# Sliding-window attention beside an MLP: row maxima by 64 queries of two heads and 320 keys, with the zeros in q's stacks

## The chip, the cores and the metric

One core of a Trainium2 chip runs the whole program. Its engines are TensorE (PE: matmuls; PEld: the loads of its weights), VectorE (DVE), ScalarE (ACT), GpSimd (POOL) and SyncE (SP), whose queue issues every DMA here. The metric is the device time of one execution in microseconds (us); several executions are timed and their median is given.

## The reference

Two branches read the same x (2048 tokens, 512 features) and are mixed by a gate per token.

```python
def _A_ref(x, wqkv, wo):
    B, S, D = x.shape
    H = 32; Dh = D // H; W = 256
    qkv = (lambda x, *d: x.transpose(*d))((x @ wqkv).reshape(B, S, 3, H, Dh), 2, 0, 3, 1, 4)
    q, k, v = qkv[0], qkv[1], qkv[2]
    scores = jnp.einsum("bhqd,bhkd->bhqk", q, k) * (Dh ** -0.5)
    idx = jnp.arange(S)
    mask = (idx[:, None] - idx[None, :] >= 0) & (idx[:, None] - idx[None, :] < W)
    scores = jnp.where(mask[None, None], scores, -1e9)
    p = _softmax(scores, axis=-1)
    o = jnp.einsum("bhqk,bhkd->bhqd", p, v)
    return (lambda x, *d: x.transpose(*d))(o, 0, 2, 1, 3).reshape(B, S, D) @ wo

def _B_ref(x, w1, b1, w2, b2):
    h = _gelu(jnp.einsum("bsd,df->bsf", x, w1) + b1)
    return jnp.einsum("bsf,fd->bsd", h, w2) + b2

g = _sigmoid((x * gate_w).sum(-1, keepdims=True))
return g * _A_ref(A_x, A_wqkv, A_wo) + (1 - g) * _B_ref(A_x, B_w1, B_b1, B_w2, B_b2)
```

A query sees its own key and the 255 before it. There are 32 heads of 16 features; the MLP has 1792 hidden units.

## The kernel before, in words

*Precision.* Matmul operands are float32r, each value as a high and a low part. `mm3` (lines 89 to 92) multiplies high by high, high by low and low by high. Attention does the same with one matmul by stacking: q and k of a head are 48 rows, 16 features each of (high, low, high) in one and of (high, high, low) in the other, in the order that `load_stack` brings them from scratch tensors SQ and SK in DRAM, one of each for every 512 tokens ("chunk").

*Heads.* A group is four heads, handled as two pairs (`pr`) of two (`s`). Rows 0 to 47 of the stacks belong to the pair's first head, rows 48 to 95 to its second. In the kernel before, `qs` holds both heads' q on top of one another, and `ks` holds each head's k apart, with zeros in the other head's 48 rows (`ks[:, pr, s]`). A matmul of the 96 rows so gives the scores of the one head whose k it takes.

*Maxima.* `att_max(g_, b, i)` (L377) computes, for 128 queries of one head, the scores against up to 384 keys (tile `sm`, three PSUM buffers), and `red` (L382) has DVE add a mask and take the maximum of each row into `M`, in one instruction whose elementwise output `jm` is thrown away. A second small instruction reads the maximum out. For every four blocks of 128 queries (`RB`), `att_rows` negates the maxima on DVE, as a high and a low part, transposes them (L393 to L397), and POOL copies them by `put` (L402) into rows 96 to 103 of `qs`. Ones in rows 96 to 103 of `ks`, written by `clear_k` from `own`, pick the two rows of the own head, so that the next matmul of the scores has the maximum already subtracted.

*Weights of attention.* `att_exp` (L417) takes 128 keys as the stationary operand and up to 384 queries as the moving one (tile `st`), ACT takes the exponential (L429), and POOL zeroes what lies outside the window (L421, L424). `att_pv` (L449) multiplies by v. Its result goes to DRAM (ND, L461), the normaliser is loaded, inverted and applied for each pair of groups (`att_norm`: den, num, RD, rb, OT), and the output projection follows at the end.

*Order.* PE, ACT, DVE and POOL run in the order in which the program is written; each engine takes its instructions in turn. A clock kept while the program is written (`now`, `tick`, `after`) decides that order: `after(ns, f)` puts `f` so many model nanoseconds later. The main loop (from line 700) goes over blocks u of 128 keys in all 8 groups, 16 to a group. The maxima run `LEAD` = 8 blocks ahead of the exponentials. In each of four turns of a block it writes one maximum, one matmul of weights and about 574 ns of dense work (QKV projections at first, then the MLP), by `fill`. DMAs stand on SP's queue in an order that the tile framework's scheduler makes; each uses one of eight semaphores in turn. Every fourth block, `att_load` brings the next chunk of q and k, over the place whose last reader is the matmul of weights eight blocks behind. The MLP's input is brought back by `load_x` (tile `mx`, L501), the weights as `raw`.

*Start.* While the QKV projections of the first three chunks run, `ks` and `qs` serve as buffers of the transposed x; `clear_k` and `load_k` then prepare `ks` piece by piece, and q follows at line 698.

Of the kernel before, what the change touches and what calls it, by code (L numbers as in the profile page):

```python
# [9 lines left out]
F32 = mybir.dt.float32  # L10
F32R = mybir.dt.float32r
BF16 = mybir.dt.bfloat16
AF = mybir.ActivationFunctionType
# [19 lines left out]
def gated_mix(ctx: ExitStack, tc: tile.TileContext, x, wqkv, wo, w1, b1, w2, b2, gate_w, out):  # L33
# [11 lines left out]
    def f32(ap):  # L45
        return ap.bitcast(F32)

    idle = sb.tile([128, 384], BF16, tag="jm", bufs=1, name="idle")
# [18 lines left out]
    mask = cp.tile([128, 384], BF16, name="mask")  # L67
    nc.gpsimd.memset(mask, 0.0)
    nc.gpsimd.affine_select(out=mask[:, 0:128], in_=mask[:, 0:128], pattern=[[1, 128]],
                            compare_op=ALU.is_ge, fill=NEG, base=-1, channel_multiplier=-1)  # L70
    nc.gpsimd.affine_select(out=mask[:, 256:384], in_=mask[:, 256:384], pattern=[[-1, 128]],
                            compare_op=ALU.is_ge, fill=NEG, base=0, channel_multiplier=1)

    own = cp.tile([128, 4], F32, name="own")
    nil = cp.tile([128, 1], F32, name="nil")
    nc.gpsimd.memset(nil, 0.0)
    nc.gpsimd.memset(own, 0.0)
    for k in (0, 1):
        nc.gpsimd.affine_select(out=own[96:104], in_=own[96:104], pattern=[[-2, 4]], compare_op=ALU.not_equal,
                                fill=1.0, base=-k, channel_multiplier=1)  # L80
    nms = cp.tile([128, RB, 32], F32R, name="nm")
# [3 lines left out]
    z = cp.tile([128, S // 128], F32, name="z")  # L85
# [99 lines left out]
    def qkv_x(t, b):  # L185

        if b == 0:
            if t < NT - 1:
                v = (ks[:, 0], ks[:, 1], qs)[t].rearrange("p a c -> p (a c)")
# [25 lines left out]
    def gate_end(t):  # L215
        sl = slice(t * NB, (t + 1) * NB)
        nc.scalar.activation(g1[:, sl], z[:, sl], AF.Exp, scale=-1.0)
# [4 lines left out]
    def gate_z(t, b):  # L222
# [3 lines left out]
        nc.vector.tensor_tensor_reduce(junk, xr, gwb, 1.0, 0.0, ALU.mult, ALU.add, z[:, nb:nb + 1])  # L226
# [48 lines left out]
    def qkv(t):  # L275
# [17 lines left out]
        for n, (kind, j) in enumerate(pieces):  # L293
# [15 lines left out]
            if t == 1 and n % 3 == 2:  # L309
                clear_k(n // 3)  # L310
            if t == 2 and n in (1, 3, 5, 7):
                clear_k(4 + n // 2)
# [456 lines left out]
```

## Time and profile before

| what | value |
|---|---|
| median of 3 timed runs | 789.53 us (787.77 to 789.83) |
| the profiled execution | 789.78 us |
| its span | 788.1 us |
| granted TensorE clock, mean | 0.995 |
| share of the span: PE, PEld, DVE, ACT, POOL | 97, 78, 66, 54, 46% |
| DMA packets | 97085, 139.66 MB |

A matmul's record goes from its start to the end of its last result, and the next one starts before that end; busy PE time is thus an upper bound on work, and distances between starts are the price. "jm", "sm", "st", "nm", "tt" are the program's tile names; L and a number is a line of the kernel. A row of a group gives the line, the engine, the operation, output<-input, partitions x elements, the count, then busy us, mean ns of one, and the idle time before it with what ended it.

### The profile page before, as it was taken

What the parts mean: (1) busy time and instruction counts of PE and PEld (TensorE: products, weight loads), DVE (VectorE), ACT (ScalarE), POOL (GpSimd) and SP (SyncE); (2) the same over time, 40 slices, a digit from 0 to 9 for tenths busy, and PEclk for the clock granted to TensorE, in tenths of its full rate; (3) what the DMA queues carried; (4) which work ended last, traced back from release to release, by engine and by line L of the source; (5) the groups of instructions that cost most, each with busy time, mean ns of one, the idle gap of its engine ahead of it and who ended that gap; (6) DMA issues with size and microseconds to landing.
All of it is one profiled execution on the core that took longest, in us unless ns stands there. A gap on an engine that the chain in (4) does not pass through costs nothing.

```text
span 788.1 us, 14535 instructions
## 1 busy us (share of the span) xinstructions
PE 768.1 (97%) x4630; PEld 618.5 (78%) x4630; DVE 521.6 (66%) x1516; ACT 429.0 (54%) x865; POOL 363.6 (46%) x701
## 2 busy tenths in 40 slices
PE   8999999989999999999999999999999999999997
PEld 5888888867888878788868867878888888777776
DVE  4533333888568857966996799668867966791353
ACT  4424433356467546755774577457646754775640
POOL 2200000047457745754765467447744863685100
PEclk9999999999999999999999999999999999999999
DMA  9985856637552653573335556533664364345882
GB/s 292 362 299 189 302 189 202 229 108 256 153 134 69 213 176 113 183 205 115 106 109 161 168 148 191 156 91 109 199 202 137 94 228 129 116 135 177 257 294 94
DMA packets 97085, 139.66 MB, mean 177 GB/s; under 512 B 32496, under 2 KB 44016, under 8 KB 97008
## 3 DMA queue, kind: packets, MB, share of 16 engines
q1 hardware_dynamic: 97008, 138.72, 55.8%
q8 instruction: 37, 0.61, 0.3%
q14 instruction: 40, 0.33, 0.1%
HBM read 83.63 MB, written 55.05 MB: 176 GB/s over the span
## 4 chain that ended last, share of the span: by engine, by line
PE 66%; DVE 5%; issue 4%; DMA 2%; ACT 2%; POOL 1%; DVEq 0%; POOLq 0%; SPq 0%
PE pv L449 10%; PE st L417 9%; PE sm L377 9%; PE y L90 7%; PE y L91 6%; PE y L92 6%; PE u L90 5%; PE u L91 4%; PE u L92 4%; DVE jm L382 2%; PE a L92 1%; DVE sqh L541 1%; PE a L90 1%; PE a L91 1%; DMA ND<-nd 1%
## 5 line engine op out<-in xcount | busy, mean ns | idle before, releaser
L382 DVE CUSTOM_DVE_ANT_0 jm<-sm,mask 128x384 bf16<-128x384 f32 (+2 forms) x512 | 269.5, 526 | 121.0 <-PE sm L377 94.2
L429 ACT ACTIVATE pt<-st 128x384 f32<-128x384 f32 (+2 forms) x512 | 232.5, 473 | 148.3 <-PE st L417 142.1
L421 POOL TENSOR_SCALAR_AFFINE_SELECT pt<-pt 128x256 f32<-128x256 f32 x256 | 117.4, 459 | 184.0 <-ACT pt L429 177.9
L377 PE MATMUL sm<-ks,qs 96*128 96x384 f32 (+2 forms) x512 | 171.2, 336 | 8.7 <-DVE M L382 7.7
L417 PE MATMUL st<-qs,ks 128*128 128x384 f32 (+2 forms) x512 | 169.2, 332 | 0.9 <-ACT pt L429 0.9
L377 PEld LDWEIGHTS sm<-ks,qs 96*128 96x128 f32 x512 | 96.8, 189 | 37.5 <-DVE M L382 19.5
L417 PEld LDWEIGHTS st<-qs,ks 128*128 128x128 f32 x512 | 97.6, 191 | 18.7 <-ACT pt L429 1.5
L424 POOL TENSOR_SCALAR_AFFINE_SELECT pt<-pt 128x256 f32<-128x256 f32 x224 | 102.5, 457 | 0.0
L553 POOL TENSOR_TENSOR h<-x1h,h 128x512 fp32r<-128x512 f32 x56 | 81.8, 1460 | 37.2 <-DVE h L550 29.4
L90 PE MATMUL y<-w,h 128*128 128x512 f32 x224 | 89.8, 401 | 0.0
L402 POOL CAST qs<-tt 8x256 fp32r<-8x256 f32 x128 | 64.7, 505 | 50.7 <-PE u L92 38.8
L91 PE MATMUL y<-w,h 128*128 128x512 f32 x224 | 88.0, 393 | 0.0
L92 PE MATMUL y<-w,h 128*128 128x512 f32 x224 | 88.0, 393 | 0.0
L449 PE MATMUL pv<-pt,vbuf 128*32 128x384 f32 (+2 forms) x1408 | 84.3, 386 | 0.0
L90 PE MATMUL u<-mx,w 128*128 128x512 f32 x196 | 79.1, 404 | 0.0
L91 PE MATMUL u<-mx,w 128*128 128x512 f32 x196 | 76.6, 391 | 0.0
L92 PE MATMUL u<-mx,w 128*128 128x512 f32 x196 | 76.5, 390 | 0.0
L449 PEld LDWEIGHTS pv<-pt,vbuf 128*32 128x32 f32 x1408 | 41.5, 110 | 41.8 <-issue 29.1
L245 DVE TENSOR_TENSOR qke<-qk,qke 128x512 fp32r<-128x512 f32 x32 | 22.1, 690 | 49.7 <-ACT qke L242 48.1
L460 ACT ACTIVATE nd<-pv 128x512 f32<-128x512 f32 x32 | 19.2, 598 | 60.1 <-PE pv L449 57.9
L242 ACT ACTIVATE qke<-qk 128x512 fp32r<-128x512 f32 x32 | 19.2, 599 | 57.7 <-PE qk L92 43.1
L92 PEld LDWEIGHTS y<-w,h 128*128 128x128 f32 x224 | 42.3, 189 | 9.4
(116 smaller groups left out, 1231.5 us busy)
## 6 DMA issues: line engine op xcount, KB each, us to landing
mx<-XT SPq DMA_DIRECT2D x24, 512.0 KB
SQ<-qke SPq DMA_DIRECT2D x16, 512.0 KB
SK<-qke SPq DMA_DIRECT2D x16, 512.0 KB
qs<-SQ SPq DMA_DIRECT2D x64, 128.0 KB
ND<-nd SPq DMA_DIRECT2D x32, 256.0 KB
ks<-SK SPq DMA_DIRECT2D x60, 128.0 KB
raw_w<-in_B_w_dram SPq DMA_DIRECT2D x28, 256.0 KB
SV<-vx SPq DMA_DIRECT2D x16, 272.0 KB
```

The lines of the kernel that those rows point to most:

```text
L90: nc.tensor.matmul(p, lh, rh, start=first, stop=False)
L91: nc.tensor.matmul(p, lh, rl, start=False, stop=False)
L92: nc.tensor.matmul(p, ll, rh, start=False, stop=last)
L377: nc.tensor.matmul(p[:, :w], qs[0:96, pr, b * 128:(b + 1) * 128], ks[0:96, pr, s, k0:k0 + w], start=True, stop=True)
L382: nc.vector.tensor_tensor_reduce(junk[:, :w], p[:, :w], mask[:, 384 - w:384], 1.0, -3e38, ALU.add, ALU.max, M[:, b % RB, i:i + 1])
L402: nc.gpsimd.tensor_copy(dst, tt[32 * i:32 * i + 8].unsqueeze(1).broadcast_to([8, 2, RB, 32]))
L417: nc.tensor.matmul(p[:, :w], ks[:, pr, s, kb * 128:(kb + 1) * 128], qs[:, pr, kb * 128:kb * 128 + w], start=True, stop=True)
L421: nc.gpsimd.affine_select(out=pt[:, :, 0:128], in_=pt[:, :, 0:128], pattern=[[0, 2], [1, 128]], compare_op=ALU.is_ge, fill=0.0, base=0, ch ...
L424: nc.gpsimd.affine_select(out=pt[:, :, 256:384], in_=pt[:, :, 256:384], pattern=[[0, 2], [-1, 128]], compare_op=ALU.is_ge, fill=0.0, base= ...
L429: nc.scalar.activation(pt[:, s, :w], p[:, :w], AF.Exp, scale=SCALE)
L449: nc.tensor.matmul(pv[32 * i:32 * i + 32, q - c * T:e - c * T], vt[:, 68 * (kb % NB) + 17 * i:68 * (kb % NB) + 17 * i + 32], pts[g_, kb, i ...
L553: nc.gpsimd.tensor_sub(h[:, 1], x1, f32(h[:, 0]))
```

## The change

The zeros move from k's stacks to q's. `ks` now holds both heads' k on top of one another, `[128, 2, S]`, and `qs` is `[128, 2, 2 * S]`: for every 64 queries it has 64 columns of the one head and 64 of the other, with zeros in the other head's rows. In a block of 128 queries the four runs of 64 columns are second head, first head, first head, second head, so that the first head's 128 columns lie together and the second head's in two runs.

`att_max` takes 128 such columns, that is 64 queries of both heads, as the stationary operand, and up to 320 keys as the moving one. There are as many of these matmuls as before. The mask is 320 wide, in two halves of partitions. `M`, `nm` and `tt` are by 64 queries and two pairs, and `put` copies 4 partitions of 512 elements where it copied 8 of 256. `att_exp` takes k of both heads in 100 rows, and picks the head by the columns of q: two runs of 64 columns out of every 256 for the second head. The ones in rows 96 to 99 of `ks` are written once, by two copies on POOL.

q is brought by `load_q`, for one pair and one head at a time: two DMAs with runs of 128 columns for the first head, four for the second (runs of 128, and of 64 at both ends). A chunk so has 12 DMAs of q where it had 4; k keeps 4 and now follows q. At the start q is loaded early and k at the end, the other way round from before.

Besides, the thrown-away output is a fixed tile of bytes, `M` and `den` have one buffer in place of two, the gate's sums lie in `g1`, and `att_rows` is due 50 model ns after its last maximum, not 900.

```diff
...
-    mask = cp.tile([128, 384], BF16, name="mask")
+    mask = cp.tile([128, 320], BF16, name="mask")
...
+    junk = cp.tile([128, 320], U8, name="junk")
...
+    nil = own[:, 2:3]
...
-    nms = cp.tile([128, RB, 32], F32R, name="nm")
+    nms = cp.tile([128, RB * 2, 32], F32R, name="nm")
...
-    qs = cp.tile([128, 2, S], F32R, name="qs")
-    ks = cp.tile([128, 2, 2, S], F32R, name="ks")
-
-    def clear_k(i):
+
+    qs = cp.tile([128, 2, 2 * S], F32R, name="qs")
+    ks = cp.tile([128, 2, S], F32R, name="ks")
+
+    def clear_q(i):
 
         pr, n = divmod(i, 4)
-        v = ks[:, pr].rearrange("p s c -> p (s c)")
-        c = 2 * pr + n // 2
-        nc.scalar.activation(v[:, n * 1024:(n + 1) * 1024], nil.broadcast_to([128, 1024]), AF.Identity,
-                             bias=own[:, c:c + 1])
+        nc.scalar.activation(qs[:, pr, n * 1024:(n + 1) * 1024], nil.broadcast_to([128, 1024]), AF.Identity, bias=nil)
...
-    def load_k(g_, c, prs):
+    def load_stack(src, high, put):
+
+        put(0, src.rearrange("d s c -> (d s) c"))
+        put(32, src[:, high])
+
+    def load_q(g_, c, prs):
+
+        need(("qk", c, g_ // 2))
+        for pr in range(prs.start, prs.stop):
+            v = f32(qs[:, pr, 2 * c * T:2 * (c + 1) * T])
+
+            def put_a(r, src):
+                dst = v[r:r + src.shape[0]].rearrange("r (n x) -> r n x", x=256)[:, :, 64:192]
+                nc.sync.dma_start(dst, src.rearrange("r (n x) -> r n x", x=128))
+
+            def put_b(r, src):
+                w = v[48 + r:48 + r + src.shape[0]]
+                nc.sync.dma_start(w[:, 192:960].rearrange("r (n x) -> r n x", x=256)[:, :, 0:128],
+                                  src[:, 64:448].rearrange("r (n x) -> r n x", x=128))
+                nc.sync.dma_start(w.rearrange("r (n x) -> r n x", x=64)[:, 0:16:15],
+                                  src.rearrange("r (n x) -> r n x", x=64)[:, 0:8:7])
+            load_stack(SQ[c][4 * g_ + 2 * pr], 1, put_a)
+            load_stack(SQ[c][4 * g_ + 2 * pr + 1], 1, put_b)
+
+    def att_load(g_, c, k_only=False):
         need(("qk", c, NC + g_ // 2))
         cs = slice(c * T, (c + 1) * T)
+        if not k_only:
+            load_q(g_, c, slice(0, 2))
         for s in range(2):
-            heads = slice(4 * g_ + 2 * prs.start + s, 4 * g_ + 2 * prs.stop - 1 + s, 2)
-            load_stack(SK[c], 0, heads, lambda r, n: ks[48 * s + r:48 * s + r + n, prs, s, cs])
...
+            src = SK[c][4 * g_ + s:4 * g_ + 3 + s:2]
+            nc.sync.dma_start(f32(ks[48 * s:48 * s + 32, :, cs]), src.rearrange("h d s c -> (d s) h c"))
+            nc.sync.dma_start(f32(ks[48 * s + 32:48 * s + 48, :, cs]), src[:, :, 0].rearrange("h d c -> d h c"))
...
     def att_max(g_, b, i):
...
-        k0 = max(b - 2, 0) * 128
-        w = (b + 1) * 128 - k0
-        pr, s = divmod(i, 2)
+        pr, half = i % 2, i // 2
+        k = 2 * b + half
+        w = min(W + 64, 64 * k + 64)
+        k0 = 64 * k + 64 - w
         p = ps.tile([128, 384], F32, tag="sm", bufs=3, name=f"sm{g_}_{b}_{i}")
-        nc.tensor.matmul(p[:, :w], qs[0:96, pr, b * 128:(b + 1) * 128], ks[0:96, pr, s, k0:k0 + w],
-                         start=True, stop=True)
...
+        nc.tensor.matmul(p[:, :w], qs[0:96, pr, k * 128:(k + 1) * 128], ks[0:96, pr, k0:k0 + w], start=True, stop=True)
         def red():
...
-            nc.vector.tensor_tensor_reduce(junk[:, :w], p[:, :w], mask[:, 384 - w:384], 1.0, -3e38,
-                                           ALU.add, ALU.max, M[:, b % RB, i:i + 1])
+            if b % RB == 0 and i == XOR:
+                Ms[g_, b // RB] = sb.tile([128, RB * 2, 2], F32, tag="M", bufs=1, name=f"M{g_}_{b}")
+            M = Ms[g_, b // RB]
+            nc.vector.tensor_tensor_reduce(junk[:, :w], p[:, :w], mask[:, 320 - w:320], 1.0, -3e38,
+                                           ALU.add, ALU.max, M[:, b % RB * 2 + half, pr:pr + 1])
...
         def put(i):
-            dst = qs[96:104, :, rb * RB * 128:(rb + 1) * RB * 128]
-            dst = dst.rearrange("r s (b i j) -> r s b i j", b=RB, i=4)[:, :, :, i]
-            nc.gpsimd.tensor_copy(dst, tt[32 * i:32 * i + 8].unsqueeze(1).broadcast_to([8, 2, RB, 32]))
+            dst = qs[96:100, :, rb * RB * 256:(rb + 1) * RB * 256]
+            dst = dst.rearrange("r s (b i j) -> r s b i j", i=4, j=32)[:, :, :, i]
+            nc.gpsimd.tensor_copy(dst, tt[32 * i:32 * i + 4].unsqueeze(1).broadcast_to([4, 2, RB * 2, 32]))
...
-        nc.tensor.matmul(p[:, :w], ks[:, pr, s, kb * 128:(kb + 1) * 128],
-                         qs[:, pr, kb * 128:kb * 128 + w], start=True, stop=True)
+        q = qs[0:100, pr, kb * 256:kb * 256 + 2 * w].rearrange("r (b u j) -> r b u j", u=4, j=64)
+        q = q[:, :, 0:4:3] if s else q[:, :, 1:3]
+        nc.tensor.matmul(p[:, :w], ks[0:100, pr, kb * 128:(kb + 1) * 128], q, start=True, stop=True)
...
-        den = sb.tile([128, 32], F32, tag="den", bufs=2, name=f"den{t}_{c}")
+        den = sb.tile([128, 32], F32, tag="den", bufs=1, name=f"den{t}_{c}")
...
     need(("v", NT - 2, NB - 1))
+    for pr in range(2):
+        nc.gpsimd.tensor_copy(ks[96:100, pr], own[96:100, pr:pr + 1].broadcast_to([4, S]))
     att_load(*chunks.pop(0), True), att_load(*chunks.pop(0), True)
...
-            after(900, att_rows, gm, bm // RB)
+            after(50, att_rows, gm, bm // RB)
```

More of the change, by code (lines that the diff above doesn't have):

```diff
@@ L12 @@
 BF16 = mybir.dt.bfloat16
+U8 = mybir.dt.uint8
 AF = mybir.ActivationFunctionType
@@ L46, in f32 @@
         return ap.bitcast(F32)
-    idle = sb.tile([128, 384], BF16, tag="jm", bufs=1, name="idle")
+    idle = sb.tile([128, 384], BF16, tag="ya", bufs=2, name="idle")
     nc.gpsimd.memset(idle, 0.0)
@@ L225, in gate_z @@
         nb = t * NB + b
-        nc.vector.tensor_tensor_reduce(junk, xr, gwb, 1.0, 0.0, ALU.mult, ALU.add, z[:, nb:nb + 1])
+        nc.vector.tensor_tensor_reduce(junk, xr, gwb, 1.0, 0.0, ALU.mult, ALU.add, g1[:, nb:nb + 1])
     def qkv_qk(t, j):
@@ L337, in gated_mix @@
     vts, Ms, pts, pvs = {}, {}, {}, {}
-    def load_stack(src, high, heads, rows):
-        nc.sync.dma_start(f32(rows(0, 32)), src[heads].rearrange("h d s c -> (d s) h c"))
-        nc.sync.dma_start(f32(rows(32, 16)), src[:, :, high][heads].rearrange("h d c -> d h c"))
-    def load_k(g_, c, prs):
+    def load_stack(src, high, put):
[16 more added lines that the diff above has]
+            load_stack(SQ[c][4 * g_ + 2 * pr + 1], 1, put_b)
```

43 lines of the change are left out of this document (14 added, 29 removed).

## The prediction

> **What bounds the kernel now.** I began with the page's busy shares, then cut the span into windows, then read the tensor engine's start times one by one.
>
> ```profile
> span 788.1 us, 14535 instructions
> PE 768.1 (97%) x4630; PEld 618.5 (78%) x4630; DVE 521.6 (66%) x1516; ACT 429.0 (54%) x865; POOL 363.6 (46%) x701
> ```
>
> The profiled execution took 789.78 us, 1.7 more than its span; the three timed runs have a median of 789.53. The sum below is made against 789.8.
>
> ```profile
> 130.00:735.00 605.00, 594.54 (x3822) 478.44 (x3824) 453.01 (x1389) 361.62 (x753) 351.46 (x664) 0.99 0.51 155
> 175.00:180.00 5.00, 3.93 (x16) 2.95 (x17) 4.57 (x12) 3.79 (x9) 4.82 (x9) 1.00 0.50 157
> 405.00:410.00 5.00, 3.65 (x17) 2.62 (x15) 5.00 (x11) 3.24 (x8) 4.81 (x7) 1.00 0.54 150
> 410.00:415.00 5.00, 4.55 (x15) 3.85 (x16) 4.20 (x14) 2.58 (x5) 2.28 (x6) 0.70 0.16 54
> 455.00:485.00 30.00, 27.97 (x183) 20.01 (x181) 28.75 (x74) 21.76 (x44) 21.20 (x33) 1.00 0.46 133
> ```
>
> These are windows; the columns are busy PE, PEld, DVE, ACT, POOL, then granted clock, DMA share, GB/s. From 130 to 735 us, the whole attention stage, PE is busy 594.5 of 605 us: whatever shortens a matmul there shortens the kernel. The exceptions are short. At 405 to 410 DVE is busy all 5.00 us and PE 3.65; then the clock is granted at 0.70. Between 455 and 485 DVE is busy 28.75 of 30. At 175 to 180 POOL is at 4.82 of 5.
>
> A busy matmul overlaps its neighbours, so its price is the distance from its start to the next start:
>
> ```profile
> 219.82 0.34 PE L377 MATMUL sm<-ks,qs 96*128 96x384 f32 x1
> 222.92 0.34 PE L377 MATMUL sm<-ks,qs 96*128 96x384 f32 x1
> 779.85 0.39 PE L90 MATMUL a<-wo,ot 128*128 128x512 f32 x1
> 781.89 0.28 PE L90 MATMUL a<-wo,ot 128*128 128x256 f32 x1
> 783.93 0.28 PE L92 MATMUL a<-wo,ot 128*128 128x256 f32 x1
> 204.17 0.22 PE L377 MATMUL sm<-ks,qs 96*128 96x128 f32 x1
> 204.23 0.40 PE L417 MATMUL st<-qs,ks 128*128 128x384 f32 x1
> ```
>
> Nine 512-column matmuls go from 779.85 to 781.89: 0.2267 us each. Seventeen of 256 columns go from there to 783.93: 0.120. Three rounds of one sm, one st and three 512s go from 219.82 to 222.92, 1.033 each; less 3 x 0.2267 that leaves 0.353, or 0.1766 for each 384-column matmul. A 128-column sm takes 0.06. So cost grows by 0.06 per 128 columns with no floor at these sizes, although each has a 128-column weight load.
>
> **The change, part by part.** The order of PE's instructions is unchanged, the new kernel issues as many matmuls, and each sm or st streams fewer columns or as many. The rows are groups by line, shapes apart: count | busy us, mean ns | idle before, and what ended it.
>
> ```profile
> L377 PE MATMUL sm<-ks,qs 96*128 96x384 f32 x448 | 154.9, 347 | 8.7 <-DVE M L382 7.7
> L377 PE MATMUL sm<-ks,qs 96*128 96x256 f32 x32 | 9.1, 283 | 0.0
> L377 PE MATMUL sm<-ks,qs 96*128 96x128 f32 x32 | 7.3, 227 | 0.0
> L382 DVE CUSTOM_DVE_ANT_0 jm<-sm,mask 128x384 bf16<-128x384 f32 x448 | 247.0, 551 | 88.3 <-PE sm L377 63.7 <-PE st L417 0.5
> L382 DVE CUSTOM_DVE_ANT_0 jm<-sm,mask 128x256 bf16<-128x256 f32 x32 | 13.5, 423 | 10.2 <-PE sm L377 9.2
> L402 POOL CAST qs<-tt 8x256 fp32r<-8x256 f32 x128 | 64.7, 505 | 50.7 <-PE u L92 38.8
> L82 POOL MEMSET nm<- 128x128 f32 x1 | 0.2, 205 | 0.1
> L84 POOL MEMSET vbuf<- 128x32 f32 x1 | 0.1, 125 | 0.0
> ```
>
> 1. *sm shrinks.* Now: 448 x 0.1766 + 32 x 0.120 + 32 x 0.06 = 84.9 us. After: 448 of 320 columns at 0.148, half way between 0.120 and 0.1766, plus 16 each of 64, 128, 192 and 256 columns, 0.30 us for such a set: 66.3 + 4.8 = 71.1. **Gain 13.8 us, on the path.** The points lie within 2 ns of a line, so 13 to 15; zero if 320 were charged like 384.
>
> 2. *st reads q in runs.* Its 384 columns are now three runs of 128 for even heads, six of 64 for odd ones, and 100 rows in place of 128. No row shows a moving operand in runs. Lower end: 0, only the count matters (128-row st and 96-row sm cost the same now); no gain below that, since the columns are the same. Next, three runs at 0.06 are 0.18: 3.4 ns more, 1.7 us over 512. Upper end: a run of 64 costs as the shortest stream seen, 0.06: six are 0.36, 0.183 more for each of 256 odd-head matmuls, 47 us. I take 1, the 384-column row being nearest, and the far end as a rival.
>
> 3. *The reductions shrink.* 320 elements interpolate to 487 ns, 64 below 551: 448 x 0.064 = 28.7 us of DVE. PE covers nearly all of it; it pays only where DVE sets the pace. There 64 ns are saved where PE saves 29, so 35 ns more per reduction: about 100 reductions in the windows around 175, 400, 470 and 700 give 3.5 us, against PE's whole wait on reductions of 7.7 us above. **I take 3;** bounds 0 and 9 (7.7 plus half of a clock window such as that after 410). The bytes in place of bf16 for the thrown-away result, and one M buffer, which DVE alone writes and reads in order, I cost at nothing; DVE's own order covers them.
>
> 4. *POOL's casts double per partition,* from 8x256 to 4x512. Bounds 505 ns (partitions counted not at all, fixed cost all) and 1010 (all by element); the two memsets give 80 ns for 96 elements, so a fixed part of some 100, and doubling the other 405 gives 910; I take 900. That is 128 x 0.4 = 51 us, to about 403 of 605 us in the stage: covered, except where POOL's queue stands on the chain of waits:
>
> ```profile
> 174.01 0.75 POOL qs L402
> 178.22 1.26 POOL h L553
> 179.51 0.69 ACT x1h L535
> ```
>
> The casts of rows sit ahead of the subtraction at 178.22, for which ACT's gelu waits, and behind it PE's next u. Four casts there, 0.4 each: **1.6 us lost**, between 0 and 2.
>
> DVE and POOL also hold each other up:
>
> ```profile
> 394.81 0.68 DVE L149 TENSOR_TENSOR w<-raw_w,w 128x512 fp32r<-128x512 f32 x1
> 407.28 1.28 POOL L553 TENSOR_TENSOR h<-x1h,h 128x512 fp32r<-128x512 f32 x1
> 407.33 1.78 DVE L149 TENSOR_TENSOR w<-raw_w,w 128x512 fp32r<-128x512 f32 x1
> ```
>
> The same DVE subtraction takes 0.68 alone and 1.78 when it starts beside POOL's at 407.28. So longer casts can hand part of the 28.7 us back; if all 51 us of them fell on DVE, point 3 would be zero or a loss. [...]
>
> 5. *Loads.* Per group and 512-token chunk, k keeps its 4 DMAs; q goes from 4 to 12, all on SP's queue, q now first. The two chunks loaded early go the same way. With 8 more issues, everything behind them on SP (k, V, normaliser and MLP loads) comes later. A window, SP's and PE's timelines, and a step of the chain of waits (the time from issue to landing):
>
> ```profile
> 180.00:185.00 5.00, 4.77 (x23) 3.66 (x22) 4.57 (x15) 4.52 (x11) 3.90 (x7) 1.00 0.78 294
> 185.13 2.28 SPq L501 DMA_DIRECT2D mx<-XT  x4
> 192.05 0.32 SPq L461 DMA_DIRECT2D ND<-nd  x1
> 192.41 0.43 SPq L342 DMA_DIRECT2D ks<-SK  x1
> 193.84 0.98 SPq L341 DMA_DIRECT2D qs<-SQ  x1
> 194.87 0.43 SPq L342 DMA_DIRECT2D qs<-SQ  x1
> 195.34 0.42 SPq L341 DMA_DIRECT2D qs<-SQ  x1
> 196.34 0.30 SPq L342 DMA_DIRECT2D qs<-SQ  x1
> 332.12 0.32 SPq L461 DMA_DIRECT2D ND<-nd  x1
> 336.74 0.30 SPq L342 DMA_DIRECT2D qs<-SQ  x1
> 344.24 0.22 PE L377 MATMUL sm<-ks,qs 96*128 96x128 f32 x1
> 459.59 2.85 DMA raw_w<-in_B_w_dram
> ```
>
> An issue takes 0.47 (194.87 to 195.34); a load of short runs lands in 2.85. Chunk 4's last load starts at 196.34, lands by about 199.2, and is first used at 204.17: margin 5.0 us. Chunk 12: 336.74, 339.6, 344.24: 4.6. Eight more issues are 3.8, so most chunks keep about a microsecond. At chunk 4 more moves: the four mx loads, now ahead of ND, stand behind it. They start near 192.5, and 2.1 MB at the 294 GB/s of the window is 7 us, to about 200; a load waits until the one eight before it has landed (eight DMA semaphores go round), so six issues and a landing follow, 205.7, where PE wants them near 202.7 (204.17 less what sm has saved). **3 us lost there, 1 elsewhere:** 4, from 0 to 10. The normaliser's loads for DVE come up to 3 us later too; DVE's shorter reductions cover that, without them it is in the upper end.
>
> 6. *The rest:* two 4x2048 copies on POOL before its first cast at about 150 us, in 38.8 us of idle (row L402): nothing, and half a row of DVE at most if late. Clearing q in place of k is the same eight ACT passes.
>
> Sum: 789.8 - 13.8 + 1 - 3 + 1.6 + 4 = **779.6 us**.
>
> **The rivals.**
> - *Cheaper:* the loads stay inside their margins and DVE's stalls go with the throttled windows they cause: 789.8 - 13.8 - 6 = 770. For it: margins of 5.0 and 4.6 against 3.8. Against: mx behind ND.
> - *POOL hands DVE's gain back:* point 3 nothing, 1.6 grows to 5: 786. For it: 4.82 of 5 at 175 us. Against: POOL at 351 of 605 over the stage.
> - *Nothing:* 320 columns cost as 384 because the weight load binds: 789.8 + 0 to 2, about 790. Against it: 0.120 at 256 columns with the same load.
> - *Slower, SP's queue sets the pace:* the strided issues take 0.98 like that at 193.84, so 12 q issues take 12 us where 4 take 2 and each of 30 chunks comes late. It decides once a chunk's loads are later by the 4.6 to 5.0 us of margin; beyond the break-even of 14/30 = 0.5 us late per chunk it is slower than before. At 1 us late: 779.6 - 4 + 30 = 805. For it: SP already waits in order behind ND. Against: raw_w, also in short runs, issues and lands like the others.
> - *Slower, short runs on PE:* 779.6 + 47 = 826, for odd heads alone. Nothing in the profile speaks for it but the absence of a row.
>
> **How the numbers follow.** Forecast 0.50 (own range 774 to 785); cheaper 0.18; POOL 0.08; nothing 0.05; SP 0.15; short runs 0.04. A measurement of this kernel tells about 0.3% (2.4 us) from no change, so faster 0.76, same 0.05, slower 0.19. The range reaches from just under the cheaper case, 768, through "nothing", to a mild form of the SP case, 796; outside stay short runs, most of SP and the tail of the cheaper case, some 0.2.
>
> **What would show it.** sm 320 to the next start at 0.148; st still 0.177 after both even and odd heads; reductions near 487 ns; casts near 850; PE idle at 405 to 410 shrunk. A wait of PE's or its weight loads' for DMA at the first sm of chunk 4 shows point 5; the same at every chunk shows the SP rival. Wrong at the root is the forecast if PE's busy share in the stage falls clearly below 98%, or if st's distance grows.

## The result, and the profile after

| kernel | median of the timed runs | ratio to before, 95% interval |
|---|---|---|
| before | 789.1 us (787.77 to 789.83, 6 runs) | |
| changed | 797.73 us (794.90 to 798.93, 6 runs) | 1.0106 [1.0086, 1.0127] |

The changed kernel is slower by 8.6 us. The forecast was 779.6, and its range ended at 796. The profiled execution took 796.15 us.

The page of the changed kernel (span and busy shares), its window over the attention stage, and its groups by line, shapes apart:

```profile
span 794.4 us, 14886 instructions
PE 763.7 (96%) x4630; PEld 608.7 (77%) x4630; DVE 509.5 (64%) x1516; ACT 428.3 (54%) x865; POOL 397.6 (50%) x704
```

```profile
130.00:735.00 605.00, 582.43 (x3766) 462.07 (x3765) 433.67 (x1382) 355.32 (x739) 376.55 (x656) 0.99 0.52 152
```

```profile
L390 DVE CUSTOM_DVE_ANT_0 junk<-sm,mask 128x320 uint8<-128x320 f32 x448 | 216.9, 484 | 85.0 <-PE sm L385 59.8 <-DVE M L390 1.0 <-PE y L92 0.5
L427 PE MATMUL st<-qs,ks 100*128 100x384 f32 x448 | 155.3, 350 | 3.8 <-ACT pt L438 2.6 <-POOL qs L410 1.1
L385 PE MATMUL sm<-ks,qs 96*128 96x320 f32 x448 | 141.9, 318 | 13.1 <-DVE M L390 12.8
L410 POOL CAST qs<-tt 4x512 fp32r<-4x512 f32 x128 | 90.2, 705 | 70.5 <-DVE tt L405 54.1 <-DVE M L390 10.9
```

The parts did what they were to do: the reduction fell from 551 to 484 ns, and PE is busy 4.4 us less. But PE stood still longer. In the stage it was busy 594.5 of 605 us and now is 582.4; its wait for the maxima (M) before sm grew from 7.7 to 12.8 us on the 320-column form alone. So the loss is not in the matmuls but in what they wait for.

The tensor engine runs the same instructions in the same order in both traces, so the starts can be laid side by side by number:

| from PE's instruction to the next in the list | before | changed |
|---|---|---|
| 0 to 900 | 200.8 us | 198.1 us |
| 900 to 1000 | 13.2 | 21.0 |
| 1000 to 4629 | 569.3 | 570.6 |

Between these two executions the net loss is 6.4 us. A hundred instructions at chunk 4, the first chunk of the second group, lose more than that, 7.8 us. Behind them the narrower matmuls gain nothing in 570 us. Both want an explanation. First chunk 4, in SP's timeline (start, time of issue) and in SP's waits between 189 and 203 us (total, times, longest):

```profile
190.02 1.75 SPq L510 DMA_DIRECT2D mx<-XT  x4
...
194.81 1.57 SPq L350 DMA_DIRECT2D qs<-SQ  x2
197.60 0.30 SPq L354 DMA_DIRECT2D qs<-SQ  x1
199.11 0.30 SPq L356 DMA_DIRECT2D qs<-SQ  x1
...
201.80 0.42 SPq L369 DMA_DIRECT2D ks<-SK  x1
202.27 0.42 SPq L374 DMA_DIRECT2D vbuf<-SV  x1
202.74 0.50 SPq L598 DMA_DIRECT2D ya<-in_B_b_dram  x1
```

```profile
SPq L350 <- DMA mx<-XT: 1.3, 2, 0.7
SPq L356 <- DMA mx<-XT: 1.2, 1, 1.2
SPq L354 <- DMA mx<-XT: 1.2, 1, 1.2
```

The q loads of lines 350 to 356 wait for the mx transfers: eight semaphores go round (100 and 102 to 108 in the trace), and an issue waits for the landing of the one eight ahead. Two of the twelve are issued ahead of the mx loads; with the other ten behind four transfers of 512 KB, the last k load goes out at 201.80. What that does on PE, on DVE, and in windows of 5 us (busy PE, PEld, DVE, ACT, POOL, granted clock, DMA share, GB/s):

```profile
201.18 0.39 PE L92 MATMUL y<-w,h 128*128 128x512 f32 x1
204.92 0.27 PE L385 MATMUL sm<-ks,qs 96*128 96x64 f32 x1 [3.35 <-DMA ks<-SK]
...
207.47 0.42 PE L385 MATMUL sm<-ks,qs 96*128 96x64 f32 x1 [1.32 <-DVE M L390]
```

```profile
206.31 0.69 DVE L607 SCALAR_TENSOR_TENSOR yo<-y,ya 128x512 f32<-128x512 f32 x1 [6.43 <-DMA ya<-in_B_b_dram]
```

```profile
200.00:205.00 5.00, 1.65 (x9) 1.16 (x8) 0.00 (x0) 0.92 (x3) 1.53 (x4) 1.00 0.59 155
205.00:210.00 5.00, 3.67 (x12) 2.69 (x12) 2.96 (x13) 0.98 (x2) 0.77 (x2) 0.62 0.77 209
210.00:215.00 5.00, 5.00 (x52) 2.51 (x52) 0.09 (x2) 1.07 (x2) 2.43 (x5) 0.69 0.14 34
```

One late load costs three times here. PE stands 3.35 us for k. The MLP's bias row `ya`, which is loaded behind the chunk, arrives later still, so DVE stands 6.43 us at L607 with the next reductions behind it, and PE waits 1.32 more for M. And in the two windows behind the stop the clock is granted at 0.62 and 0.69 in the mean, where it is at 1.00 from 195 to 205 us and from 215 to 220; by these two means about 3.5 us of full clock are lost (an estimate). That the stop brings the clock down is the author's reading of this order in time; what does it no run shows.

The losses after chunk 4 have another place. SP's timeline around the first normaliser of the second group, first in the kernel before and then in the changed one, DVE's and PE's next to it in the changed one, and the waits of DVE for den (total, times, longest) before and after:

```profile
261.73 0.32 SPq L461 DMA_DIRECT2D ND<-nd  x1
...
265.44 0.73 SPq L479 DMA_DIRECT2D den<-ND  x1
```

```profile
265.99 0.32 SPq L470 DMA_DIRECT2D ND<-nd  x1
266.35 0.44 SPq L356 DMA_DIRECT2D qs<-SQ  x1
...
274.07 0.50 SPq L598 DMA_DIRECT2D ya<-in_B_b_dram  x1
274.62 0.72 SPq L488 DMA_DIRECT2D den<-ND  x1
```

```profile
277.34 0.35 DVE L494 RECIPROCAL den<-den 128x32 f32<-128x32 f32 x1 [2.28 <-DMA den<-ND]
```

```profile
278.10 0.41 PE L385 MATMUL sm<-ks,qs 96*128 96x320 f32 x1 [0.95 <-DVE M L390]
```

```profile
DVE den L485 <- DMA den<-ND: 2.5, 1, 2.5
```

```profile
DVE den L494 <- DMA den<-ND: 14.9, 8, 3.5
```

In the kernel before, SP issues 7 other DMAs between the store of nd and the load of den, and 3.7 us pass; in the changed one it issues 15, 13 of them q's and k's, and 8.6 us pass. den lands late, DVE stands at the reciprocal, the reductions of sm stand behind it, sm's PSUM buffers stay full, and PE waits. Five times behind chunk 4 PE's wait for M follows such a stop of DVE at the reciprocal: 0.95, 0.60, 1.32, 1.57 and 1.08 us, from 278 to 605 us (at the third, the last thing DVE waited for is put down to a load of weights on the same queue).

### The profile page after: what moved, and what is told of

It reads as the page before. It is cut to its first block, busy times and chain, and to the rows that moved or that the text cites. A ratio compares the mean times of both kernels' runs of the same rounds, so it can differ in the third digit from the quotient of the medians.

```text
span 794.4 us, 14886 instructions
## 1 busy us (share of the span) xinstructions
PE 763.7 (96%) x4630; PEld 608.7 (77%) x4630; DVE 509.5 (64%) x1516; ACT 428.3 (54%) x865; POOL 397.6 (50%) x704
## 4 chain that ended last, share of the span: by engine, by line
PE 59%; DVE 7%; DMA 4%; issue 4%; POOL 2%; SPq 2%; ACT 1%; DVEq 0%; POOLq 0%
PE pv L458 9%; PE st L427 9%; PE sm L385 7%; PE y L90 6%; PE y L91 5%; PE y L92 5%; PE u L90 5%; PE u L91 4%; PE u L92 4%; DVE junk L390 3%; DMA den<-ND 2%; PE a L92 2%; PE a L90 2%; PE a L91 2%; DVE sqh L550 1%
## 5 line engine op out<-in xcount | busy, mean ns | idle before, releaser
L390 DVE CUSTOM_DVE_ANT_0 junk<-sm,mask 128x320 uint8<-128x320 f32 (+4 forms) x512 | 237.4, 464 | 119.0 <-PE sm L385 91.3
L427 PE MATMUL st<-qs,ks 100*128 100x384 f32 (+2 forms) x512 | 171.3, 338 | 3.8 <-ACT pt L438 2.6
L385 PE MATMUL sm<-ks,qs 96*128 96x320 f32 (+4 forms) x512 | 157.7, 310 | 17.8 <-DVE M L390 14.1
L410 POOL CAST qs<-tt 4x512 fp32r<-4x512 f32 x128 | 90.2, 705 | 70.5 <-DVE tt L405 54.1
L427 PEld LDWEIGHTS st<-qs,ks 100*128 100x128 f32 x512 | 97.8, 191 | 22.7 <-ACT pt L438 3.4
L562 POOL TENSOR_TENSOR h<-x1h,h 128x512 fp32r<-128x512 f32 x56 | 84.6, 1510 | 26.4 <-DVE h L559 20.8
L90 PE MATMUL u<-mx,w 128*128 128x512 f32 x196 | 80.3, 410 | 0.0
L91 PE MATMUL u<-mx,w 128*128 128x512 f32 x196 | 78.1, 399 | 0.0
L92 PE MATMUL u<-mx,w 128*128 128x512 f32 x196 | 77.0, 393 | 0.0
L550 DVE SCALAR_TENSOR_TENSOR sqh<-sqh,x1h 128x512 f32<-128x512 f32 x56 | 48.8, 871 | 3.3 <-ACT sqh L547 3.2
```

Source lines behind the costliest of these rows:

```text
L90: nc.tensor.matmul(p, lh, rh, start=first, stop=False)
L91: nc.tensor.matmul(p, lh, rl, start=False, stop=False)
L92: nc.tensor.matmul(p, ll, rh, start=False, stop=last)
L385: nc.tensor.matmul(p[:, :w], qs[0:96, pr, k * 128:(k + 1) * 128], ks[0:96, pr, k0:k0 + w], start=True, stop=True)
L390: nc.vector.tensor_tensor_reduce(junk[:, :w], p[:, :w], mask[:, 320 - w:320], 1.0, -3e38, ALU.add, ALU.max, M[:, b % RB * 2 + half, pr:pr ...
L410: nc.gpsimd.tensor_copy(dst, tt[32 * i:32 * i + 4].unsqueeze(1).broadcast_to([4, 2, RB * 2, 32]))
```

## The experiments

Three theories stood at first. **A:** in the changed kernel all tiles from `nm` on lie 32 bytes off a multiple of 64 in their partition (in the kernel before they lie on it), and the dense 128x512 matmuls of the attention stage follow each other some 6 ns later; the place might be the cause. **L:** the loads are late. **P:** POOL's wider casts and DVE hold each other up.

**e1_align64**

```diff
-    own = cp.tile([128, 3], F32, name="own")
     junk = cp.tile([128, 320], U8, name="junk")
...
+    own = f32(nms)[:, 0, 8:11]
```

> The changed kernel with its constant `own` moved into unused columns of the normaliser tile `nm` and its own 32 bytes gone, so that nm, vbuf, qs, ks, the weights, h, mx and pt all lie 32 bytes lower: in the changed kernel they lie at 32 modulo 64 bytes of a partition, in the kernel before and here at 0 modulo 64. The same instructions in the same order otherwise. Theory A (place in memory): in the changed kernel the dense 128x512 matmuls of the attention stage follow each other 6 ns (L90) and 9 ns (L91) later than before, some 6 us in all, because of the place of the tiles; here those distances go back to 0.227 us and the time falls by 6 us, from 797.7 to about 792. Theory L (late loads of q and of den) and theory P (POOL's casts and DVE hold each other up): within 1 us of 797.7.

**e2_before32** (the kernel before)

```diff
-    nil = cp.tile([128, 1], F32, name="nil")
+    nil = cp.tile([128, 9], F32, name="nil")[:, 0:1]
```

> The kernel before, with a tile of one column made nine columns wide, so that everything allocated behind it lies 32 bytes higher, at 32 modulo 64 as in the changed kernel. Nothing else. Theory A: slower by 5 us, about 794 against 789.1, with the dense matmuls of the attention stage 6 to 9 ns further apart. Theories L and P: 789.1, ratio 1.000 within 0.002.

Measured: 798.55 us, ratio 1.0101 [1.0079, 1.0123], with the tiles back in place, and 789.63, ratio 1.0005 [0.9987, 1.0022], with those of the kernel before moved. Theory A falls, in both directions.

**e3_few_loads**

```diff
-        for pr in range(prs.start, prs.stop):
...
+        for s in range(2):
+            src = SQ[c][4 * g_ + 2 * prs.start + s:4 * g_ + 2 * prs.stop - 1 + s:2]
+            v = f32(qs[:, prs, 2 * c * T:2 * c * T + T])
+            nc.sync.dma_start(v[48 * s:48 * s + 32], src.rearrange("h d s c -> (d s) h c"))
+            nc.sync.dma_start(v[48 * s + 32:48 * s + 48], src[:, :, 1].rearrange("h d c -> d h c"))
```

> The changed kernel, but the two heads of q are loaded by 4 DMAs a chunk instead of 12, each row in one run of 512 numbers into the first half of the chunk's columns instead of in runs of 64 and 128; this leaves out the interleaving of the two heads, so the maxima and the exponents are of other numbers than the reference's. Bytes, matmuls and reductions stay as they are. Theory L: the 3.5 and 1.5 us waits at the first sm matmuls of chunk 4 go, DVE's waits for den (14.9 us in 8) fall to under 8 us, and the time falls by 5 to 11 us, to 787 to 793. Theory A: at most 1 us. Theory P: at most 1 us.

Measured: 782.15 us, ratio 0.9901 [0.9885, 0.9916]: 15.6 us faster than the changed kernel, where theory L had 11 at most. Two groups of waits of this run (DVE's for den, PE's for M), to be read against 14.9 and 14.1 us in the changed kernel:

```profile
DVE den L494 <- DMA den<-ND: 1.1, 2, 0.7
PE sm L385 <- DVE M L390: 6.9, 8, 1.9
```

Laid beside this run by the numbers of PE's instructions, in one traced execution of each, the changed kernel loses 7.8 us at chunk 4 and 8.0 behind it. Of the 8.0, the five places named above make 1.17, 0.87, 1.59, 1.83 and 1.35 us, 6.8 in all. That ties the loss behind chunk 4 to den's load.

**e4_half_cast**

```diff
-            dst = qs[96:100, :, rb * RB * 256:(rb + 1) * RB * 256]
+            dst = qs[96:100, 0:1, rb * RB * 256:(rb + 1) * RB * 256]
...
```

> The changed kernel with POOL's casts of the maxima writing one of the two pairs of heads alone (4x256 numbers each instead of 4x512), so the rows of maxima of the other pair stay what the load left there; all else is as it was. POOL falls by 128 casts times half of 705 ns, some 45 us. Theory P: the time falls by 3 to 6 us, and the 7 us of waits of sm for M shrink to before's 7.7 us. Theories A and L: within 1 us of 797.7.

Measured: 798.10 us, ratio 1.0101 [1.0080, 1.0122]. Theory P falls as to the time. As to the engines it is right; DVE's cast of h in the kernel before, the changed one and this one (count, busy us, mean ns):

```profile
L550 DVE CAST h<-x1h 128x512 fp32r<-128x512 f32 x56 | 27.2, 486 | 0.1
```

```profile
L559 DVE CAST h<-x1h 128x512 fp32r<-128x512 f32 x56 | 29.2, 522 | 0.1
```

```profile
L559 DVE CAST h<-x1h 128x512 fp32r<-128x512 f32 x56 | 27.4, 488 | 0.1
```

With half the cast, 34 of the 36 ns go, and the kernel is no faster.

Next, what it is about the loads: their number, or their short runs.

**e7_q12_long**

```diff
...
+            for s in range(2):
+                src = SQ[c][4 * g_ + 2 * pr + s]
+                for r in ((0, 32),) if s == 0 else ((0, 16), (16, 32)):
+                    nc.sync.dma_start(v[48 * s + r[0]:48 * s + r[1]], src.rearrange("d s c -> (d s) c")[r[0]:r[1]])
+                for r in ((0, 16),) if s == 0 else ((0, 8), (8, 16)):
+                    nc.sync.dma_start(v[48 * s + 32 + r[0]:48 * s + 32 + r[1]], src[r[0]:r[1], 1])
```

> The changed kernel with q still loaded by 12 DMAs a chunk, but each row in one run of 512 numbers into the first half of the chunk's columns (the rows of the second head split between two DMAs), which leaves out the interleaving of the two heads as the run with 4 DMAs did; 2 KB packets instead of 256 and 512 B. Theory L1 (it is the number of DMAs: each waits on SP until the eighth one ahead of it has landed, and each is issued behind the last): 796 to 799 us, with the waits at the first sm matmuls of chunk 4 still 4 to 5 us. Theory L2 (it is the short runs, more packets): 781 to 784 us, as with 4 DMAs.

Measured: 796.90 us, ratio 1.0077 [1.0050, 1.0103]. It is the number: twelve DMAs of long rows cost, within the uncertainty, what twelve of short runs cost.

**e9_before_q12** (the kernel before)

```diff
-            heads = slice(4 * g_ + s, 4 * g_ + 3 + s, 2)
-            load_stack(SQ[c], 1, heads, lambda r, n: qs[48 * s + r:48 * s + r + n, :, cs])
+            for pr in range(2):
+                src, q = SQ[c][4 * g_ + 2 * pr + s], f32(qs[48 * s:48 * s + 48, pr, cs])
+                rows = src.rearrange("d s c -> (d s) c")
+                for r in ((0, 32),) if s == 0 else ((0, 16), (16, 32)):
+                    nc.sync.dma_start(q[r[0]:r[1]], rows[r[0]:r[1]])
+                for r in ((0, 16),) if s == 0 else ((0, 8), (8, 16)):
+                    nc.sync.dma_start(q[32 + r[0]:32 + r[1]], src[r[0]:r[1], 1])
```

> The kernel before, with its q loads cut by rows into 12 DMAs a chunk instead of 4; same bytes, same long rows, nothing else. Theory L1 (the number of DMAs on SP's queue): 796 to 806 us, 7 to 16 us more than 789, with a wait at the first sm matmul of chunk 4. Rival (it needs the changed kernel's other parts to be late): within 2 us of 789.

Measured: 810.57 us, ratio 1.0272 [1.0258, 1.0286], 21 us slower and beyond what was expected. Its PE at chunk 4, the clock behind it, and DVE's waits for den:

```profile
205.47 0.30 PE L382 MATMUL sm<-ks,qs 96*128 96x128 f32 x1 [1.49 <-DMA qs<-SQ]
210.50 0.48 PE L382 MATMUL sm<-ks,qs 96*128 96x128 f32 x1 [3.80 <-DVE M L387]
```

```profile
210.00:215.00 5.00, 4.50 (x27) 3.02 (x31) 2.38 (x13) 0.98 (x2) 1.96 (x5) 0.50 0.54 164
```

```profile
DVE den L490 <- DMA den<-ND: 14.2, 8, 4.6
```

So the eight DMAs more need nothing else of the change to be late. Nor do the single buffers of `den` and `M` explain the waits: this kernel has two of each and waits for den as the changed one does (14.9 us in 8), while e3_few_loads has one of each and waits 1.1 us. Why the same eight cost 21 us here and some 15 there the runs don't show.

Two attempts to keep them and move the wait:

**b3_early**

```diff
-LPOS = 0
+LPOS = 3
```

> The changed kernel with each chunk's loads issued one block of 128 queries earlier (some 4.5 us), nothing else. Theory L: the 12+4 DMAs are late by at most 5 us at a chunk's first sm matmul, so most of that waiting goes: 786 to 792 us. Rival: SP is a queue in order, so the loads sent earlier wait at its head for the last st matmul that reads the old chunk, and hold up den, rb and the weights behind them: 797 to 805 us.

Measured: 797.35 us, ratio 1.0103 [1.0086, 1.0120]: the rival's case. From PE's 900th to its 1000th instruction it took 13.5 us, hardly more than the kernel before; all of that was lost again later, where it took 580.7 us for the changed kernel's 570.6. DVE's waits for den were still 12.0 us in 7.

**e10_rcp_late**

```diff
-        after(NORM, rcp), after(3 * NORM, mul)
+        after(1.6 * NORM, rcp), after(3 * NORM, mul)
```

> The changed kernel with the normaliser's reciprocal put four reductions later in DVE's order (RD and rb follow it), nothing else. Theory D (beside chunk 4, the loads cost time by keeping den's load waiting on SP, so that DVE stands at the reciprocal and the reductions of sm stand behind it): DVE's waits for den (14.9 us in 8) fall under 6 us, sm's waits for M (14.1 us) by 4 us or more, and the time by 3 to 7 us, to 791 to 795. Rival (the whole of SP's queue is late, and what is not waited for at den is waited for at rb, ya or the weights): within 1.5 us of 797.7.

Measured: 804.00 us, ratio 1.0194 [1.0172, 1.0217]. Neither expectation came: theory D had a gain, and its rival at most 1.5 us of difference. The waits for den left the list, others of the same engine took their place, and PE's wait for M stayed (total, times, longest):

```profile
DVE num L499 <- DMA rb<-RD: 11.3, 5, 4.5
DVE yo L607 <- DMA ya<-in_B_b_dram: 10.3, 4, 6.5
DVE num L499 <- DMA qs<-SQ: 5.0, 1, 5.0
PE sm L385 <- DVE M L390: 15.0, 15, 3.5
```

This fits a queue that is late as a whole, in which the load of DVE's that is needed first shows it. The edit isn't clean, though: the multiplication by rb kept its place, so that 6300 model ns were left for RD and rb between the reciprocal and it, where there were 9000. The remedy of theory D fails; its account of the waits is not refuted by that.

**b1_rows48** and **b2_rows48d** take the loads away without leaving anything out of the computation. Both store a projection tile's high part a second time, so that the 48 rows of a head lie in DRAM as they are read; a chunk then takes 6 DMAs of q and 2 of k. b1_rows48's stores against those of the changed kernel:

```diff
-    SQ = [dr.tile([H, 16, 2, T], F32, name=f"SQ{t}") for t in range(NT)]
+    SQ = [dr.tile([H, 48, T], F32, name=f"SQ{t}") for t in range(NT)]
...
-            nc.sync.dma_start(dst[8 * i:8 * i + 8].rearrange("h d s c -> (h d) s c"), f32(e))
+            to = dst[8 * i:8 * i + 8]
+            nc.sync.dma_start(to[:, 0:32].rearrange("h (d s) c -> h d s c", s=2), f32(e))
+            nc.sync.dma_start(to[:, 32:48], f32(e[:, h]))
```

and b2_rows48d's against b1_rows48's:

```diff
-    SQ = [dr.tile([H, 48, T], F32, name=f"SQ{t}") for t in range(NT)]
+    SQ = [dr.tile([H, 16, 3, T], F32, name=f"SQ{t}") for t in range(NT)]
...
-            to = dst[8 * i:8 * i + 8]
-            nc.sync.dma_start(to[:, 0:32].rearrange("h (d s) c -> h d s c", s=2), f32(e))
-            nc.sync.dma_start(to[:, 32:48], f32(e[:, h]))
+            to = dst[8 * i:8 * i + 8].rearrange("h d s c -> (h d) s c")
+            nc.sync.dma_start(to[:, 0:2], f32(e))
+            nc.sync.dma_start(to[:, 2], f32(e[:, h]))
```

> The changed kernel with q's and k's 48 rows of a head (32 of the two parts, 16 of the high part again) laid down in DRAM as they are read, by a second store DMA for each projection tile (32 more DMAs of 256 KB in the first 150 us); then a chunk's loads are 6 DMAs for q and 2 for k, 8 in all as in the kernel before, with the runs of 64 and 128 numbers and the whole computation as in the changed kernel. Theory L1: 780 to 785 us, plus what the 32 stores cost in the projection stage (0 to 3 us). Theory L2: 795 to 799 us.

> As b1_rows48 (8 loads a chunk, the whole computation), but the 48 rows of a head lie in DRAM as 16 times 3 (part 0, part 1, the high part again), so that a store's outer dimension is 128 rows instead of 8 heads. Theory S (b1_rows48 lost its 62 us in the projection stage because each of its stores reached only 8 or 9 of the 16 DMA engines and took 13 to 17 us): the loss goes, the stores land in 3 to 5 us, and the time is 780 to 786 us. Rival: it is the 8 MB more of stores and 32 more DMAs themselves; then still over 810 us.

Measured: b1_rows48 855.11 us, ratio 1.0825 [1.0792, 1.0859]; b2_rows48d **782.12 us, ratio 0.9909 [0.9895, 0.9922]**, the fastest kernel here that computes everything. The window from 20 to 60 us of b1 and of b2 (columns as above):

```profile
20.00:60.00 40.00, 37.09 (x164) 29.91 (x163) 14.79 (x30) 13.46 (x25) 4.90 (x7) 0.96 0.60 201
```

```profile
20.00:60.00 40.00, 40.00 (x187) 33.07 (x187) 17.20 (x35) 15.93 (x29) 5.29 (x10) 1.00 0.99 375
```

With the same stores to make, 201 GB/s move in the one and 375 in the other: with stores laid out as 8 heads by 16 features 0.60 of the DMA engines' time is busy in this window, with 128 rows 0.99. By the packets' times, 8 or 9 packets are in flight at once for 64% of it in b1, and 16 or 17 for 77% in b2. The shares say the same in the mean: 0.60 of 16 engines is 9.6, and 0.99 is 15.8. How the layout of a store sets that number the runs don't show.

**b4_before_rows48** (the kernel before, its scratch tensors and stores as in b2_rows48d)

```diff
-        nc.sync.dma_start(f32(rows(0, 32)), src[heads].rearrange("h d s c -> (d s) h c"))
-        nc.sync.dma_start(f32(rows(32, 16)), src[:, :, high][heads].rearrange("h d c -> d h c"))
+        nc.sync.dma_start(f32(rows(0, 48)), src[heads].rearrange("h d s c -> (d s) h c"))
```

> The kernel before with the 48 rows of a head laid down in DRAM as they are read, as in b2_rows48d, so 4 loads a chunk (2 of q, 2 of k) instead of 8. If the loads on SP already cost the kernel before something (its den waits of 2.5 us, its slack of 3.4 us at the nearest chunk): 785 to 788. If they are hidden there: 789 within 1 us, and b2_rows48d's 782.1 is the change's own gain of 7 us.

Measured: 788.44 us, ratio 0.9990 [0.9974, 1.0006]. In the kernel before, eight loads a chunk are hidden; fewer bring nothing. With the rows laid down in this way on both sides, the change itself is worth 6.3 us (782.12 against 788.44).

The last question is why the narrower sm is worth so little even when the loads are in time. In both traces three dense matmuls follow each pair of sm and st. By the starts between 180 and 715 us (some 370 of each), the medians in the kernel before are 0.227 us for each of the three; in the changed kernel 0.233, 0.236 and 0.229. Four runs looked for the cause.

**e5_st128**

```diff
-        q = qs[0:100, pr, kb * 256:kb * 256 + 2 * w].rearrange("r (b u j) -> r b u j", u=4, j=64)
+        q = qs[0:128, pr, kb * 256:kb * 256 + 2 * w].rearrange("r (b u j) -> r b u j", u=4, j=64)
...
-        nc.tensor.matmul(p[:, :w], ks[0:100, pr, kb * 128:(kb + 1) * 128], q, start=True, stop=True)
+        nc.tensor.matmul(p[:, :w], ks[0:128, pr, kb * 128:(kb + 1) * 128], q, start=True, stop=True)
```

> The changed kernel with st over 128 rows instead of 100 (the 28 rows more are zeros in q's stacks), as in the kernel before. Theory K (the weights of 100 rows make the dense matmuls that follow slower): the distance of the 128x512 matmuls in the attention stage goes back from 0.233 to 0.227 us, and the time falls by 6 us to about 792. Otherwise: 797.7 within 1 us, and 0.233 as it is.

**e6_st_runs**

```diff
-        q = q[:, :, 0:4:3] if s else q[:, :, 1:3]
+        q = qs[0:100, pr, kb * 256 + s * w:kb * 256 + (s + 1) * w]
```

> The changed kernel with st reading q in one run of 384 instead of runs of 64 or 128 with gaps, which leaves out that the scores are of the right head and query; order, sizes and rows as they were. Theory R (the strided read is what slows the matmuls around it): dense distances back to 0.227, 5 to 6 us less, about 792. Otherwise 797.7 within 1 us, st's own distance 0.177 instead of 0.178.

Measured: 798.71, ratio 1.0093 [1.0063, 1.0124], and 797.36, ratio 1.0084 [1.0054, 1.0113]. Neither brings 0.227 back: the medians are 0.232, 0.233, 0.232 with 128 rows and 0.233, 0.236, 0.229 with one run. On the way it is seen that the read in runs costs st itself nothing: its median distance to the next start is 0.178 us in the changed kernel and 0.178 with one run.

**e8_wide_few** (from e3_few_loads)

```diff
-        k0 = 64 * k + 64 - w
+        x = 64 if w == W + 64 and k > 4 else 0
+        k0 = 64 * k + 64 - w - x
...
-        nc.tensor.matmul(p[:, :w], qs[0:96, pr, k * 128:(k + 1) * 128], ks[0:96, pr, k0:k0 + w], start=True, stop=True)
+        nc.tensor.matmul(p[:, :w + x], qs[0:96, pr, k * 128:(k + 1) * 128], ks[0:96, pr, k0:k0 + w + x], start=True, stop=True)
...
-            nc.vector.tensor_tensor_reduce(junk[:, :w], p[:, :w], mask[:, 320 - w:320], 1.0, -3e38,
+            nc.vector.tensor_tensor_reduce(junk[:, :w], p[:, x:x + w], mask[:, 320 - w:320], 1.0, -3e38,
```

> The kernel with 4 q DMAs a chunk (e3_few_loads), with sm again 384 columns wide (64 keys more than the reduction reads, which leaves their scores out). What the narrower sm alone is worth. By the pitch of sm (0.177 against 0.146 us, some 448 matmuls): 13.8 us slower, 796 us. By the distance from one sm to the next over sm, st and three dense matmuls (1.033 us in the kernel before, 1.021 in the changed one, because the dense ones got 6, 9 and 2 ns longer): 5 to 8 us slower, 787 to 790 us, with the dense distances back at 0.227.

**e11_wide_128** (e8_wide_few with the edit of e5_st128)

> e8_wide_few (4 q DMAs, sm 384 wide) with st over 128 rows again, so that sm and st have the shapes that they have in the kernel before. Theory P (the dense matmuls keep 0.227 us only beside that pair of shapes, and lose 5 ns beside any other): dense distances back at 0.227, and 1 to 3 us faster than e8's 787.7. Rival (something else of the change slows them: the runs of st's read, POOL's or DVE's traffic): 0.233 as in e8, 787 to 788.5.

Measured: e8 787.68 us, ratio 0.9978 [0.9965, 0.9991], 5.5 us slower than with 320 columns, within the lower of its two expectations, though the dense distances did not come back (medians 0.233, 0.233, 0.228); e11 786.83, ratio 0.9968 [0.9955, 0.9980]. PE's timeline of e8 and then of e11, the first of three dense matmuls and the sm behind them:

```profile
217.34 0.40 PE L90 MATMUL y<-w,h 128*128 128x512 f32 x1
...
218.04 0.34 PE L385 MATMUL sm<-ks,qs 96*128 96x384 f32 x1
```

```profile
219.34 0.39 PE L90 MATMUL u<-mx,w 128*128 128x512 f32 x1
...
220.02 0.34 PE L385 MATMUL sm<-ks,qs 96*128 96x384 f32 x1
```

The three take 0.70 us in e8 and 0.68 in e11, and there the medians are 0.227 for each. The dense matmuls keep 0.227 in all three medians beside this pair of shapes, 384 columns on 96 rows and 384 on 128, and at none of the others tried (320 or 384 columns, 100 rows; 320 columns, 128 rows). In e8 the medians hide two kinds of rounds: of 367, 105 last 1.030 us from sm to sm and 112 last 1.050, where more than half of e11's last 1.033 or 1.034. Of that run's theories, P holds for the distances. The time, 0.9 us less than e8's with intervals that overlap, decides nothing. What in the engine does this the runs don't show.

## Why the prediction was wrong, by its own steps

The direction was wrong through step 5, and the size of the gain through step 1. The sign that the prediction named for being wrong at the root did come: PE's busy share in the stage fell from 98.3% to 96.3% (582.43 of 605 us). And without step 5 its sum is 775.6 us, while e3 and b2, where the loads are in time, take 782.1: 6.5 us of the error lie outside the loads.

For step 1, three rounds of the changed kernel in PE's timeline, with the starts of the first and the last sm:

```profile
273.61 0.31 PE L385 MATMUL sm<-ks,qs 96*128 96x320 f32 x1
...
276.67 0.31 PE L385 MATMUL sm<-ks,qs 96*128 96x320 f32 x1
```

1. *sm shrinks, 13.8 us.* The distance from a 320-column sm to the next start was forecast at 0.148; at 0.146 it came in so. Mis-sized was its worth: widening sm again costs 5.5 us (e8 against e3), not 13.8. The prediction took the price of a 512-column matmul, 0.2267, as a constant and looked only at sm's own distance. The dense neighbours give back more than half: three rounds of sm, st and three dense matmuls take 3.06 us where they took 3.10, 13 ns less a round, while sm alone saves 31. At 448 rounds that is 6 us.
2. *st in runs, 1 us lost.* Right within the uncertainty: e6, with one run, is at 797.36 against 797.73. The rival of 47 us falls with it.
3. *Reductions, 487 ns, 3 us.* 484 ns. But PE's wait for M, on which the 3 us drew, is 6.9 us in e3 and 7.7 in b2 against 7.7 before, so that at most 0.8 came of it there. e11, which keeps the reductions, the casts, the runs and the rest of the change but has the old matmul shapes and few loads, is 2.3 us faster than before; steps 2 to 4 and 6 together were forecast at 0.4 of gain. Not separated further.
4. *Casts, 900 ns, 1.6 us lost.* 705 ns, and e4 shows no loss from the wider cast. The hold-up between POOL and DVE was there: DVE's cast of h, with one input, takes 522 ns here where it took 486, and 488 in e4. What in the engines makes it no run shows.
5. *Loads, 4 us lost, from 0 to 10.* 15.6 us (e3), all but what lies within the uncertainty from the number of DMAs (e7). At chunk 4 the mechanism was foreseen, with the mx loads ahead and eight semaphores, and the wait for the load too: 3 us forecast, 3.35 measured. But that stretch lost 7.8: not counted were the `ya` behind the chunk's loads, which held DVE for 6.43 us, and the clock at 0.62 and 0.69 afterwards. "1 elsewhere" is the step that failed most: from PE's 1000th instruction on the changed kernel takes 8.0 us more than e3, 6.8 of them at five places where DVE stands for den. The prediction set the late loads against the slack of q and k themselves, which did suffice behind chunk 4, and of the normaliser's loads it said that "DVE's shorter reductions cover that". They don't: a reduction that is 67 ns shorter gives DVE no help while it stands in front of a reciprocal whose den is still behind 13 loads, and its waits for den went from 2.5 to 14.9 us. The rival "SP's queue sets the pace" named the right queue, but as a delay of each chunk at PE, not of what DVE waits for; PE waited for a chunk's load once, 3.35 us at chunk 4, and not at every chunk.
6. *The rest, nothing.* No run contradicts it. The single buffers of `den` and `M` don't make the waits (e9, e3); what they cost by themselves, and the earlier `att_rows`, was not tried.

Set end to end, the runs from the kernel before over e11, e8 and e3 to the changed kernel give sizes: 2.3 us gained by what e11 keeps of the change; 0.9 lost, within its uncertainty, by the 100 rows; 5.5 gained by the width; 15.6 lost by the loads. These are the differences along one chain of runs, so they add up by construction, and their sum confirms nothing. What confirms the largest of them is that b2, which computes everything, comes out at e3's time, and that e9, without the rest of the change, loses 21 us to the same number of loads.

## What to carry to other kernels

Count the DMAs that an edit adds to an in-order queue with few in flight (here SP's, with eight semaphores), and price them at what stands behind them in the queue, not at the data they bring: ask for each later load which engine stands still for it and which instructions stand behind that one. Moving the load or its consumer only moved the wait here (b3_early 797.35 us, e10_rcp_late 804.00); taking the DMAs away, by laying data down in DRAM in the order in which it is read, brought back all of it (b2_rows48d 782.12). Putting these loads on another engine's queue, or k ahead of q again, was not tried. And price a matmul in its sequence, by a whole round from start to start, since its neighbours' distances depended here on its shape: 0.227 us for each of the three dense matmuls in e11, and 0.233, 0.233 and 0.228 in e8, where st has 100 rows in place of 128.

## What the runs showed of the hardware that was not expected

- 128x512 matmuls follow each other every 0.227 us among themselves and beside one pair of shapes, and every 0.228 to 0.236 (medians) beside the others tried.
- Reading the moving operand in runs of 64 or 128 columns with gaps costs st nothing: 0.178 us with runs and 0.178 with one run of 384.
- Tiles 32 bytes off a multiple of 64 cost nothing: ratio 1.0005 [0.9987, 1.0022] (e2_before32).
- With stores whose outer dimension is 8, the DMA engines moved 201 GB/s from 20 to 60 us, where they moved 375 with 128 (b1_rows48, b2_rows48d).
